# The same instructions of a routed-attention and SoLU kernel in another written-out order on every engine

## The chip, the cores and the metric

The kernel runs on one core of a Trainium2 chip. Its engines are TensorE (PE in the profile; its weight loads are shown apart as PEld), VectorE (DVE), ScalarE (ACT), GpSimd (POOL) and SyncE (SP), which here only issues transfers. The metric is the time of one execution on the device, in microseconds (us); smaller is better.

## What is computed

Attention in which a query sees only the keys of its own cluster, over 4 batches, 8 heads, 768 positions and head width 64, and behind it a feed-forward layer with a softmax gate on 3072 tokens (512 wide, 1024 inside):

```python
def _attn_ref(q, k, v, centroids):
    q_n, k_n, c_n = ...            # each row divided by its norm
    q_assign = np.argmax(np.einsum('bhsd,hcd->bhsc', q_n, c_n), axis=-1)   # 16 clusters
    k_assign = np.argmax(np.einsum('bhsd,hcd->bhsc', k_n, c_n), axis=-1)
    mask = q_assign[:, :, :, None] == k_assign[:, :, None, :]
    scores = np.where(mask, np.matmul(q, k.transpose(0, 1, 3, 2)) / np.sqrt(D), -1e9)
    attn = softmax(scores)
    return np.matmul(attn, v)

def _moe_ref(x, w_in, w_out, g_ln):
    h = x @ w_in
    solu = h * softmax(h)
    ln = (solu - mean(solu)) / np.sqrt(var(solu) + 1e-06) * g_ln
    return ln @ w_out
```

Inputs and output are float32; the large products run in bf16.

## The kernel before

The work is cut into named tasks, each of one engine. A task is added with what it needs and a function that issues its instructions. The engine's order is not found by a scheduler at build time: it is written out by hand as a text, `Weave.ORDER`, one per engine, in which a word such as `ld4` means the next four tasks of the kind `ld` on that engine, taken in the order in which they were added. Within a kind the order is fixed by that; the text sets only how the kinds are interleaved. `Weave.run` places the tasks so and issues them; every engine then works its own list strictly in order, and semaphores make it wait where an input isn't ready.

The kinds that matter below, with the lines of their instructions:

- On SP: `ld` loads of q and k (lines 381 and 406; from batch 1 on, four strips of 96 KB make one operand of a head pair), `lv` loads v of a head pair (line 536, 384 KB into tile `vf`), `lo` and `li` the weights (574, 558), `tx` transposes the attention output x of one or two row tiles into `xT` (704), `tu` transposes the gated activation u of a row tile into `uT` (760), `ou` stores a row tile of the output (827), `pl` places cluster rows (519).
- On PE: `wm` and `fl` are idle matmuls on a zeroed tile that nobody reads (844); `tp` turns the first batch's q and k (393); `cl` compares with the centroids (457 and 452); `S` is one bank of scores (615); `V` multiplies the exponentials with v (644); `h` and `y` are the two products of the feed-forward layer (736 and 800), each in four parts; `ptx` and `ptu` transpose by PE at the end (714, 724).
- On ACT: `E` is the exponential of one score bank (625), `ex` that of the feed-forward layer (748), `sc` scales the output (815 or 817), `xa` copies turned q and k out of PSUM (400).
- On DVE: `tb mx oh ot` find the cluster of each row (466, 479, 491, 501), `xt` turns q and k of later batches (414), `N` normalises attention output (669), `hm u bn ag` are the maximum, the gate and the variance of the feed-forward layer (742, 755, 766, 770).
- On POOL: `ca` and `cv` cast operands (440, 442, 541), `pl` and `bl` place and blank cluster rows, `at` and `al` make the scale of a row tile (776, 782, 785).

There are 24 row tiles of 128 tokens. Tile f goes through `h` (PE), `hm` (DVE), `ex` (ACT), `u` (DVE), `tu` (SP), `y` (PE), `sc` and `ou`. Scores run in a ring of three PSUM banks and their exponentials in a ring of nine tiles, `vf` has three buffers and `raw` (q and k as loaded) eight. Attention of later batches and the feed-forward layer of earlier ones are interleaved on all engines from about 40 us on.

Of the kernel before, what the change touches and what calls it, by code (L numbers as in the profile page):

```python
# [22 lines left out]
class Weave:  # L23
# [3 lines left out]

    ORDER = {}
    ORDER["SP"] = """
        ld4 si ld4 lg lv ld2 lv ld3 lo ld lv ld2 lv ld2 lo2 ld3 lo ld4 li ld li3 tx ld lv  # L30
        ld3 lv tx ld3 tu ld8 tu tx ld5 lv tu ld3 ou ld3 tu ou ld2 lv ld10 tu ld6 ou tx lv
        ld2 tu ld ou ld2 tx ld tu ld2 lv ld2 tx ld tu ou2 ld lv ld8 tu2 ld ou ld7 pl ou ld
        lv2 ld3 tu lv tx ou tu lv pl ld4 ou2 tx lv tu tx ou tu pl2 tu2 tx tu tx ou2 tx ou tu
        tx2 ou tu2 ou2 tu2 ou6
    """
    ORDER["POOL"] = """
        po zo ca3 z ca pl ca bl pl2 ca bl ca pl sg cv z ca3 cv ca pl cv pl2 ca2 pl gs pl2 cv
        ca z ca z2 cv ca2 pl3 ca2 pl cv pl3 ca bl ca wi4 cv at ca2 pl2 cv ca pl ca pl cv al
        at2 ca cv bl ca al ca pl al pl bl pl cv at pl ca4 at ca2 al ca pl2 bl pl2 cv2 ca3 al
        at pl2 bl pl2 ca pl al ca3 at cv at pl ca pl2 ca2 pl al cv2 bl cv2 pl2 ca pl al pl  # L40
        at al at pl2 ca3 at al bl cv pl2 bl cv2 ca3 pl5 al cv3 at al ca2 cv ca cv ca2 at ca2
        pl ca al pl2 at2 pl3 at ca cv al at2 al2 at2 al at al3 at al2 at2 al2
    """
    ORDER["PE"] = """
        fl wm fl tp2 cp fl2 cl tp fl tp fl4 cl S3 tp2 S cq tp S tp S tp S2 tp S tp S2 cl S2
        tp S V S V S V S gt V S V2 S cl S3 V3 S tp S tp S tp S2 tp V S V2 S2 cl S4 V S V3 S3
        V S V S V S V S cl S3 V3 S2 V S su S4 V2 S V S V su S4 V2 S V S V me S4 V2 ptx V2 S4
        cl S2 V2 S h S V S V S h3 S2 V2 S V S2 V h2 V S V S V S h S V S h S3 V S h S V3 h S
        V2 S h S h S2 y S y2 S y S V S V S V cl h S V S h S2 V2 S h2 S3 y4 V2 h V S V S h S
        V h V S h2 S y3 S2 y V3 h S3 cl V2 S V S y S2 y2 S3 V3 S y S2 V3 S2 cl S V S2 V2 S h  # L50
        S2 V2 S V S h S2 V2 cl V2 S3 y2 S V S2 V y S2 y V2 S3 h2 S V h S h S2 V h S V S V y2
        S h V y2 S2 V S h3 S cl V S2 V2 S h V cl S3 h2 V y V S3 y2 V S h V3 S y S h S2 h2 S3
        V2 y h S V S2 y V3 y S3 h3 y S3 V3 S h S V S V cl S V S h S cl V2 S3 y V2 S y S2 y
        V2 S3 h y V S3 V h V2 S3 cl S2 V2 S y3 S2 y S V3 S V S y S2 V S V3 S2 y2 S3 y V2 S2
        h V2 S3 h3 S V S2 V y S V h2 V2 S y S2 y V y S h2 S3 cl h V S2 V3 S h V2 S3 h2 S y
        S2 V h S2 V y2 V4 S3 y h S2 h V h V S V S y2 S3 V3 h2 S2 h2 S2 y2 S V S h2 S V3 S2 h
        S h S2 V S y V2 S V y2 S2 h2 S2 h2 V2 S2 V2 y S2 h V2 h V S2 h S V h S3 V2 h y S V
        y3 V h3 S2 y3 S2 y h2 V2 h y h y3 h V h V y4 h ptx h y4 h2 y3 h2 y ptu2 y6 ptu y ptu
        y5
    """  # L60
# [1240 lines left out]
```

## Time and profile before

| | |
|---|---|
| time, median of 3 runs | 222.88 us (222.58 to 223.67) |
| span of the profiled execution, first to last instruction | 221.0 us |
| what lies around the span, by the median | 1.9 us |
| PE busy | 213.4 us (97%) |
| DVE, ACT, POOL busy | 197.3, 191.0, 130.1 us (89%, 86%, 59%) |
| moved by DMA | 38.67 MB, mean 175 GB/s |

The listing gives the three times without saying which execution was profiled, so the span is set beside the median. A row of the profile names the line, the engine, the operation and out<-in by the program's tiles; times are from the span's start. SPq is SP's queue of issues: a row's length there is how long SP was held by the issue, not how long the transfer took.

### The profile page before, as it was taken

The page shows a single profiled execution, that of the slowest core. Times are in us where ns is not written, and L with a number is a line of the kernel's source. Part 1 is how long each engine was busy: PE and PEld are TensorE (multiplying, and loading weights), DVE is VectorE, ACT ScalarE, POOL GpSimd, SP SyncE. Part 2 cuts the span into 40 slices and gives each one's busy share as a digit, 9 for nine tenths or more (in the row PEclk, how much of TensorE's full clock was granted, in tenths as well). Part 3 has the DMA queues.
Part 4 walks back from the last instruction along what each step waited for, and adds up shares of the span by engine and source line. Part 5 has one row for each costly group of instructions (what it writes and reads, how often), then busy time and mean ns, then how long its engine had stood idle before and what let it go on. Part 6 is the DMA issues. An engine that isn't in the chain of part 4 may idle for free.

```text
span 221.0 us, 6580 instructions
## 1 busy us (share of the span) xinstructions
PE 213.4 (97%) x2392; PEld 148.3 (67%) x2424; DVE 197.3 (89%) x356; ACT 191.0 (86%) x372; POOL 130.1 (59%) x251
## 2 busy tenths in 40 slices
PE   7999999999999999999999999999999999999993
PEld 4667766767766687775677776777677677755452
DVE  3899998999999999998998989887999889888982
ACT  2799999989988999998899899999899998983363
POOL 3699989933845999637667634953895403022331
PEclk9999999999999999999999999999999999999999
DMA  6999988979999979999999896599930434396723
GB/s 147 346 279 236 281 197 223 274 159 164 176 175 209 192 157 141 204 215 176 202 221 162 189 177 169 123 210 208 237 59 19 89 63 130 90 134 169 176 78 142
DMA packets 125167, 38.67 MB, mean 175 GB/s; under 512 B 114504, under 2 KB 120656, under 8 KB 125136
## 3 DMA queue, kind: packets, MB, share of 16 engines
q1 hardware_dynamic: 123392, 37.73, 82.5%
q10 hardware_dynamic: 1744, 0.52, 1.0%
q8 instruction: 19, 0.31, 0.6%
q14 instruction: 12, 0.10, 0.1%
HBM read 23.11 MB, written 6.29 MB: 133 GB/s over the span
## 4 chain that ended last, share of the span: by engine, by line
PE 88%; DMA 3%; ACT 2%; DVE 2%; issue 2%; POOL 0%; ACTq 0%; DVEq 0%
PE sps L615 27%; PE yps L800 17%; PE hreg L736 16%; PE ops L644 15%; PE csc L457 4%; DMA uT<-u 3%; PE hreg L393 2%; ACT e L625 2%; PE idle_p L844 1%; PE hreg L615 1%; PE csc L452 1%; PE hreg L583 1%; PE hreg L800 1%; DVE u L755 1%; PE hreg L593 0%
## 5 line engine op out<-in xcount | busy, mean ns | idle before, releaser
L625 ACT ACTIVATE e<-sps 128x512 bf16<-128x512 f32 (+1 forms) x278 | 144.4, 609 | 9.6 <-PE sps L615 8.4
L615 PE MATMUL sps<-qk 80*128 80x256 bf16 (+5 forms) x616 | 92.4, 264 | 0.6 <-DVE qk L523 0.3
L615 PEld LDWEIGHTS <-qk 80*128 80x128 bf16 (+1 forms) x636 | 60.3, 121 | 25.7 <-issue 8.0
L644 PEld LDWEIGHTS <-e 128*128 128x128 bf16 x1134 | 50.0, 97 | 12.0 <-issue 1.9
L644 PE MATMUL ops<-v,e 128*128 128x65 bf16 x1134 | 55.0, 193 | 0.1
L736 PE MATMUL hreg<-w_in_sb,xT 128*128 128x512 bf16 x172 | 48.9, 379 | 1.2 <-issue 0.2
L800 PE MATMUL yps<-w_out_c,uT 128*128 128x512 bf16 x172 | 46.5, 379 | 0.9 <-DMA uT<-u 0.4
L523 POOL COPY qk<-oht 32x384 f32<-32x384 f32 (+1 forms) x48 | 24.0, 500 | 16.2 <-DVE oht L501 14.1
L755 DVE TENSOR_TENSOR u<-e_sb,hreg 128x1024 bf16<-128x1024 bf16 (+1 forms) x25 | 29.2, 1170 | 4.4 <-ACT e_sb L748 4.2
L748 ACT ACTIVATE e_sb<-hreg,nmax 128x1024 bf16<-128x1024 f32 x24 | 27.0, 1124 | 5.8 <-DVE nmax L742 5.7
L742 DVE TENSOR_REDUCE nmax<-hreg 128x1 f32<-128x1024 f32 x24 | 29.1, 1211 | 3.0 <-PE hreg L736 2.8
L766 DVE BATCH_NORM_STATS2 bs<-u 128x6 f32<-128x512 bf16 x48 | 31.5, 678 | 0.1
L800 PEld LDWEIGHTS <-uT 128*128 128x128 bf16 x200 | 18.3, 97 | 12.2 <-DMA uT<-u 0.5
L440 POOL CAST qk<-xt 64x768 bf16<-64x768 f32 (+1 forms) x30 | 24.4, 814 | 3.2 <-DVE xt L400 1.7
L442 POOL TENSOR_SCALAR qk<-xt 64x768 bf16<-64x768 f32 (+1 forms) x31 | 25.1, 809 | 2.0
L782 POOL TENSOR_SCALAR esq<-es,mv 128x1 f32<-128x1 f32 x24 | 8.7, 362 | 29.3 <-DVE mv L770 21.3
L736 PEld LDWEIGHTS <-xT 128*128 128x128 bf16 x192 | 16.7, 97 | 10.3 <-issue 1.3
L414 DVE STREAM_TRANSPOSE xt<-raw 128x768 f32<-128x768 f32 x24 | 22.6, 952 | 0.0
L669 DVE TENSOR_TENSOR x<-ops,den 128x256 bf16<-128x256 f32 (+1 forms) x39 | 18.9, 486 | 1.3
L776 POOL TENSOR_SCALAR es<-esum 128x1 f32<-128x1 f32 x24 | 5.3, 222 | 25.1 <-ACT e_sb L748 24.7
L541 POOL CAST v<-vf 128x384 bf16<-128x384 f32 x27 | 13.9, 528 | 5.6 <-DMA vf<-in_v_dram 4.9
L785 POOL TENSOR_TENSOR alpha<-esq,halves 128x1 f32<-128x1 f32 x24 | 13.7, 570 | 2.0
(86 smaller groups left out, 186.2 us busy)
## 6 DMA issues: line engine op xcount, KB each, us to landing
vf<-in_v_dram SPq DMA_DIRECT2D x16, 384.0 KB, 5.2
out_dram<-y SPq DMA_DIRECT2D x23, 256.0 KB, 2.6
raw<-in_q_dram SPq DMA_DIRECT2D x50, 96.0 KB, 3.5
raw<-in_k_dram SPq DMA_DIRECT2D x50, 96.0 KB, 3.5
w_g<-in_moe_w_out_dram SPq DMA_DIRECT2D x4, 512.0 KB, 6.5
w_st<-in_moe_w_in_dram SPq DMA_DIRECT2D x4, 512.0 KB, 5.8
raw<-in_q_dram SPq DMA_DIRECT2D x3, 384.0 KB, 6.1
raw<-in_k_dram SPq DMA_DIRECT2D x3, 384.0 KB, 6.6
```

The lines of the kernel that those rows point to most:

```text
L440: VEC[e].tensor_copy(dst, src)
L442: VEC[e].tensor_scalar(dst, src, scalar1=inv_C, scalar2=1.0, op0=Alu.mult, op1=Alu.mult)
L523: ins = VEC[e].tensor_copy(dst.bitcast(F32), src.bitcast(F32).unsqueeze(1) .to_broadcast([NB, 2, n // 2]))
L615: ins = nc.tensor.matmul(sps_[n, k][:, c0:c0 + w], side(b, h // 2, 1, h % 2, keys)[r], side(b, h // 2, 0, h % 2, slice(s0 * P, s0 * P + w) ...
L625: ins = nc.scalar.activation(es[n, k][:, :w], sps_[n, k][:, :w], Act.Exp, scale=exp_scale, bias=-exp_scale)
L644: nc.tensor.matmul(opss[g][:, s, :VW], es[n, k][:, c0:c0 + P], v1[slot(b, h // 2)][:, h % 2, kt, :VW], start=(kt == 0), stop=(kt == n_t - 1))
L736: uses(nc.tensor.matmul(hreg[:, at(f, f2)[1], :], xTs[f][:, dc, :], w_in_sb[:, dc, f2 * FF2:(f2 + 1) * FF2], start=(dc == 0), stop=(dc == ...
L742: uses(nc.vector.tensor_reduce(ff[f, "nmax"][:], pair_of(f), axis=AXY, op=Alu.max, negate=True), *both(f))
L748: uses(nc.scalar.activation(ff[f, "e"][:], pair_of(f), Act.Exp, bias=ff[f, "nmax"][:], accum_out=ff[f, "esum"][:]), *both(f))
L755: uses(nc.vector.tensor_tensor(ff[f, "u"][:, at_], ff[f, "e"][:, at_], pair_of(f)[:, at_], op=Alu.mult), *banks)
L766: nc.vector.bn_stats(ff[f, "bs"][:, f2, :], ff[f, "u"][:, f2, :])
L800: ins = nc.tensor.matmul(dst, ff[f, "uT"][:, at(f, f2)[0] * (n_fc // 2) + c, :], w_out_c[:, fc, cols], start=(fc == chunks[0]), stop=(fc = ...
```

## The change

Only the five texts of `ORDER` differ. The tasks, their functions, their needs, their engines, the tiles and the number of buffers are the same, so every engine has exactly the same instructions, in another order. The kinds' words stand for the same tasks in both, since within a kind on an engine the sequence is unchanged. Two lines of the diff, the start of SP's and of PE's text:

```diff
     ORDER["SP"] = """
-        ld4 si ld4 lg lv ld2 lv ld3 lo ld lv ld2 lv ld2 lo2 ld3 lo ld4 li ld li3 tx ld lv
...
+        ld4 si ld3 lv ld lg ld lv ld9 lv ld lo2 ld lv ld2 lo2 ld4 li4 ld tx ld3 lv ld2 tx lv
...
     ORDER["PE"] = """
-        fl wm fl tp2 cp fl2 cl tp fl tp fl4 cl S3 tp2 S cq tp S tp S tp S2 tp S tp S2 cl S2
...
+        fl8 wm tp2 cp tp cl tp cl fl S2 tp2 cq S3 tp2 S tp S2 tp S cl S2 tp S V gt S tp S2 V
```

**SP, around the transpositions of u of tiles 3 to 5.** The rows are SP's transfers in their order; `raw` is a strip of q or k, `vf` a load of v, `uT` and `xT` the transpositions, `out_dram` a store. Before, the piece begins with the load of v of pair 3 of batch 1 and the `uT` is that of tile 4, the `xT` that of tiles 6 and 7, and the last `uT` that of tile 5:

```order
L536 DMA vf<-in_v_dram 128x2x384
L406 DMA raw<-in_k_dram 32x24x32 x4
L406 DMA raw<-in_q_dram 32x24x32 x4
L406 DMA raw<-in_k_dram 32x24x32 x2
L760 DMA_TRANSPOSE uT<-u 128x8x128
L406 DMA raw<-in_k_dram 32x24x32 x2
L406 DMA raw<-in_q_dram 32x24x32 x4
L827 DMA out_dram<-y 128x512
L704 DMA_TRANSPOSE xT<-x 128x8x128
L536 DMA vf<-in_v_dram 128x2x384
L406 DMA raw<-in_k_dram 32x24x32 x2
L760 DMA_TRANSPOSE uT<-u 128x8x128
```

Now, from the load of the same v on; the first `uT` is that of tile 3, the second that of tile 4, and the `xT` of tiles 6 and 7 follows four strips behind the last row, the `uT` of tile 5 three strips behind that:

```order
L536 DMA vf<-in_v_dram 128x2x384 x2
L406 DMA raw<-in_q_dram 32x24x32
L827 DMA out_dram<-y 128x512
L406 DMA raw<-in_k_dram 32x24x32
L760 DMA_TRANSPOSE uT<-u 128x8x128
L406 DMA raw<-in_k_dram 32x24x32 x3
L406 DMA raw<-in_q_dram 32x24x32 x4
L536 DMA vf<-in_v_dram 128x2x384
L406 DMA raw<-in_k_dram 32x24x32 x3
L827 DMA out_dram<-y 128x512
L760 DMA_TRANSPOSE uT<-u 128x8x128
L536 DMA vf<-in_v_dram 128x2x384
```

Three loads of v (pairs 0, 1 and 2 of batch 2) have moved ahead of the transposition of x for tiles 6 and 7, and one strip of q has moved behind it. Two loads of v have moved ahead of the transposition of u of tile 5, and none behind.

**PE, at the start.** The idle matmuls write `idle_p`; `hreg<-ident_f,raw` turns q and k, `csc` compares with the centroids, `sps` is the first bank of scores. Before, from the last 512-wide idle matmul on:

```order
L844 MATMUL idle_p<-w_out_c 128x512
L844 LDWEIGHTS w_out_c
L844 MATMUL idle_p<-w_out_c 128x256
L393 MATMUL hreg<-ident_f,raw 128x128 x6
L890 MATMUL cps<-ident_f,w_in_sb 128x128
L844 LDWEIGHTS w_out_c
L844 MATMUL idle_p<-w_out_c 128x256
L844 LDWEIGHTS w_out_c
L844 MATMUL idle_p<-w_out_c 128x256
L457 MATMUL csc<-xt,c_bd 32x192 x4
L393 MATMUL hreg<-ident_f,raw 128x128 x3
```

Now, from the same matmul on:

```order
L844 MATMUL idle_p<-w_out_c 128x512
L393 MATMUL hreg<-ident_f,raw 128x128 x6
L890 MATMUL cps<-ident_f,w_in_sb 128x128
L393 MATMUL hreg<-ident_f,raw 128x128 x3
L457 MATMUL csc<-xt,c_bd 32x192 x4
L393 MATMUL hreg<-ident_f,raw 128x128 x3
L457 MATMUL csc<-xt,c_bd 32x192 x4
L844 LDWEIGHTS w_out_c
L844 MATMUL idle_p<-w_out_c 128x256
L615 LDWEIGHTS qk_99
L615 MATMUL sps<-qk_99 128x384
```

Eight of the nine 256-wide idle matmuls now stand at the head, ahead of the six 512-wide ones (before it was one ahead and one behind), and the first comparison with the centroids stands behind nine turns instead of six.

More of the change, by code (lines that the diff above doesn't have):

```diff
@@ L35 @@
+        ld2 tu ld8 tx tu ld3 lv ld3 tu ld ou ld4 lv2 ld ou ld tu ld7 lv ld3 ou tu lv ld4 tx
+        ld3 tu ld3 tx ou ld4 tu ld2 tx lv ld2 tu ld6 ou ld3 lv ou tu ld5 ou ld lv tu ld3 pl
+        tu ld ou lv ld ou tx lv tx ld ou tu ld pl ld pl ou tu tx tu2 pl ou tu ou tx tu tx ou
+        tx ou tx tu2 tx ou2 tu ou tu2 ou6
     """
     ORDER["POOL"] = """
-        po zo ca3 z ca pl ca bl pl2 ca bl ca pl sg cv z ca3 cv ca pl cv pl2 ca2 pl gs pl2 cv
-        ca z ca z2 cv ca2 pl3 ca2 pl cv pl3 ca bl ca wi4 cv at ca2 pl2 cv ca pl ca pl cv al
@@ L39 @@
[L39 to L42, printed above, removed]
+        po ca3 pl zo bl ca2 pl sg pl2 bl ca2 z ca cv2 ca2 cv ca pl2 ca pl ca gs ca2 pl ca
+        pl2 ca2 z ca pl cv pl2 z cv2 ca wi pl z pl wi pl wi2 pl2 cv ca bl pl ca pl ca at2 cv
@@ L43 @@
+        ca pl al ca cv ca al bl z ca cv ca2 cv pl at pl al pl bl at pl ca4 cv pl2 al at pl
+        cv2 pl bl ca al cv pl2 cv pl2 at al ca cv ca2 bl ca2 at ca pl2 ca pl2 ca bl ca al at
+        pl2 al ca cv2 pl3 at pl cv ca at cv ca pl bl ca cv at pl2 ca al ca pl cv2 ca pl al
+        ca bl pl3 ca al at ca2 at ca al cv ca pl ca cv pl al at pl ca pl2 ca cv ca pl at ca
+        al at2 al3 at3 al at al at al3 at al at al
     """
     ORDER["PE"] = """
-        fl wm fl tp2 cp fl2 cl tp fl tp fl4 cl S3 tp2 S cq tp S tp S tp S2 tp S tp S2 cl S2
@@ L46 @@
[L46 to L57, printed above, removed]
@@ new lines @@
+        S2 h S h S2 V2 h S3 V2 h S V2 y h S2 y2 S2 y S V4 S cl S V2 S2 h S h S2 cl V4 S3 y2
+        S2 y S y S2 V4 S3 h2 S h2 S3 V h y S V3 h S y S2 y h S y S h S V cl S2 h V5 cl S2 h
+        S h2 S3 h V3 y S2 h y S V3 y S2 y S h S2 V3 S2 h S y S2 V3 y2 S y S V2 h S3 V cl S2
+        V3 h S2 h S h S h S2 V2 S V2 cl S2 V S V y S y S2 V2 y S3 V h y S3 V3 h S2 h S cl S3
+        V y4 S3 V3 y2 S2 V2 S V2 S2 y S y S V4 S2 h2 S3 h2 S2 h S h S2 V6 S y2 S2 y S h S y
+        S V h S2 V cl S3 h2 y S V4 y S2 h2 S3 V3 y S y S V3 h2 S3 h2 S2 h S y S V4 y h S3 V2
@@ L71 @@
-        ag2 bn tx hm bn sc u bn ag hm bn tu ag u2 bn2 ag sc
+        cn xa cb ca tb mx oh ot pl2 tb mx oh ot cf xa3 cv xa2 tb xa mx oh gk ot ca N tb xa
+        mx pl xa oh ot xa N xt2 tb cv mx N tb pl oh ca ot N mx N oh pl N ot sk xt2 N ce2 tx
+        ce2 N ce2 N ce tb ce mx hm N oh u ot bn2 N hm xt2 u bn N ag hm bn sc xt u ag tb N xt
+        mx oh bn2 ot hm ag N xt cv u sc bn2 xt N tb mx xt oh hm ot N ag u bn sc bn xt2 N tb
+        hm tb cv N mx oh mx ag u ot oh bn N bn ag hm ot xt u xt N xt bn hm tb bn ag u mx tb
@@ L72 @@
+        N hm oh xt bn mx u N ot bn sc xt hm ag oh N u xt ot bl bn xt tb N mx bn oh hm bn ot
+        tb ag mx N u bn xt bn xt ag bn sc oh N tb hm ag sc N ot u mx N bn oh xt bn N ag ot
+        ca hm sc u N bn xt hm bn tb bl mx u N bl bn hm oh bn ag u ag ot N hm cv bl bn u bn2
+        hm N u ag N sc hm bn N bn u bn2 ag hm N ag u bn2 hm N bn ag u ag N hm bn2 u bn2 hm
+        sc u N bn ag tx ag hm bn sc u bn ag hm tu bn ag u2 bn2 ag sc
     """
     ORDER["ACT"] = """
-        wa xa3 pl ca E2 xa E8 pl E6 xa E11 xa E49 ex E10 ex E6 ca E4 ex E8 ex E3 sc E5 ca E2
@@ L75 @@
-        ex E25 ex E9 sc E6 ex E5 sc E2 ex E9 ex E8 ex E9 sc E6 ex E18 ex E21 ex E5 sc E3 ex
-        E9 ex E7 sc E2 ex E7 ex E8 ex E7 ex E6 sc E ex E2 sc E3 ex E2 sc ex sc ex sc ex tu
-        sc tu2 sc2 oz
+        wa xa3 ca pl E2 xa E5 pl E8 xa E12 xa E47 ca E3 ex E11 ex E8 ex E11 sc E3 ex E6 ca
+        E9 ex E13 ex E8 sc E6 ex E5 sc E2 ex E9 ex E12 ex E3 sc E12 ex E18 ex E18 ex E7 sc
+        E3 ex E9 ex E2 sc E5 ex E7 ex E8 ex E8 ex E2 sc E4 ex E3 sc E2 ex sc E3 ex sc ex sc
+        ex sc tu3 sc2 oz
```

22 lines of the change are left out of this document (7 added, 15 removed).

## The prediction

> **What bounds the kernel now.** I read the page's busy times and its chain of work first, then the chain piece by piece, then the stages, then SP's own queue.
>
> The page's span, its busy line, and the shares of the chain that ended last:
>
> ```profile
> span 221.0 us, 6580 instructions
> PE 213.4 (97%) x2392; PEld 148.3 (67%) x2424; DVE 197.3 (89%) x356; ACT 191.0 (86%) x372; POOL 130.1 (59%) x251
> PE 88%; DMA 3%; ACT 2%; DVE 2%; issue 2%; POOL 0%; ACTq 0%; DVEq 0%
> ```
>
> PE holds 88% of the chain, so no order can beat PE's own work by much. How much that is comes from pieces of the chain in which PE runs without a gap (start us, length us, what, number of matmuls):
>
> ```profile
> 58.54 0.86 PE yps L800 x4
> 61.30 0.78 PE csc L457 x8
> 65.59 0.66 PE sps L615 x6
> 165.36 0.73 PE ops L644 x24
> ```
>
> A matmul of the feed-forward products takes 0.215 us, one of the scores 0.11, one with v 0.030, a comparison of eight 0.78. Over the order that makes 192 x 0.215 = 41 for `h`, 41 for `y`, 636 score matmuls (36 banks of the last batch are cut in four, at half the length each) 62, 1152 x 0.030 = 35 for `V`, 17 comparisons 13, and some 14 for the turns, the weight sums and the idle matmuls: 206 us. The span is 15 us longer. About 3.3 of the 15 are the first matmuls at half pace, 2 more are waits before the first score, and 4 lie behind the last matmul, so waits inside the body can't be much over 5 us. That is the most that a new order can win; what it can lose has no such limit.
>
> The second resource is the transfer queue. Three stages (us, length, busy of each engine with its count, granted clock, DMA share, GB/s):
>
> ```profile
> 60.00:80.00 20.00, 19.68 (x217) 13.56 (x220) 19.29 (x34) 18.02 (x34) 13.28 (x26) 1.00 1.04 194
> 80.00:100.00 20.00, 19.43 (x253) 14.82 (x255) 19.32 (x37) 19.32 (x39) 13.41 (x25) 1.00 0.99 172
> 160.00:180.00 20.00, 19.74 (x246) 14.79 (x249) 17.53 (x30) 19.38 (x38) 11.24 (x22) 1.00 0.24 47
> ```
>
> Between 60 and 100 us the 16 DMA engines are full (1.04 and 0.99), at 160 they are not (0.24). And SP, which issues nearly all transfers, never rests there (start us, length us; `raw` is a strip of q or k, `vf` a load of v):
>
> ```profile
> 75.31 0.47 SPq L536 DMA_DIRECT2D vf<-in_v_dram  x1
> 75.83 4.92 SPq L406 DMA_DIRECT2D raw<-in_k_dram  x4
> 80.79 2.23 SPq L406 DMA_DIRECT2D raw<-in_q_dram  x4
> 83.07 1.42 SPq L406 DMA_DIRECT2D raw<-in_k_dram  x2
> 84.59 1.37 SPq L760 DMA_TRANSPOSE uT<-u  x1
> 86.01 1.20 SPq L406 DMA_DIRECT2D raw<-in_k_dram  x2
> 87.25 2.84 SPq L406 DMA_DIRECT2D raw<-in_q_dram  x4
> 90.13 0.60 SPq L827 DMA_DIRECT2D out_dram<-y  x1
> 90.83 1.28 SPq L704 DMA_TRANSPOSE xT<-x  x1
> 92.21 0.53 SPq L536 DMA_DIRECT2D vf<-in_v_dram  x1
> 92.79 1.03 SPq L406 DMA_DIRECT2D raw<-in_k_dram  x2
> 93.92 2.14 SPq L760 DMA_TRANSPOSE uT<-u  x1
> ```
>
> Each row begins within 0.15 us of the end of the one before. No transfer waits for its data: it waits for its turn on SP. So a transposition is issued when SP comes to it, and whatever is put ahead of it delays it. How close its readers stand (the issue to the landing of that `xT`, then the first matmul that reads it, then the `uT` of tile 5 and its reader, from the chain):
>
> ```profile
> L704 SPq DMA_TRANSPOSE xT<-x x1: 1281/1281/1281, 90.8 to 90.8; - x1
> DMA to landing us min/median/max: 3.5/3.5/3.5
> 94.73 0.81 PE L736 MATMUL hreg<-w_in_sb,xT 128*128 128x512 bf16 x3
> 93.92 5.55 DMA uT<-u
> 99.52 1.04 PE yps L800 x4
> L800 PE MATMUL yps<-w_out_c,uT 128*128 128x512 bf16 x172 | 46.5, 379 | 0.9 <-DMA uT<-u 0.4
> ```
>
> The `xT` issued at 90.83 lands at 94.3 and is read at 94.73: 0.4 us to spare. The `uT` of tile 5 is the only transfer of the body in the chain: it lands at 99.5, and PE waited for it about 0.5 us (the group of line 800 has 0.9 of idle time in all, 0.4 of it for `uT`).
>
> **The change, part by part.** All work is the same; only waits can differ. One execution was profiled, with a span of 221.0; the median of the runs is 222.88, so I add 1.9 to a span.
>
> *Loads of v moved ahead of transpositions (SP).* The `xT` of tiles 6 and 7 gets three `vf` ahead of it and loses one strip; the `uT` of tile 5 gets two `vf`. The price of a `vf`: at the 194 GB/s of the stage, 384 KB take 2.0 us, a strip of 96 KB 0.5. SP's rows give the bounds. At 75.31 the issue itself takes 0.47, which is all it costs if the queue has room; but the four strips behind it take 4.92 where the next four take 2.23, so it costs up to 0.47 + 2.69 = 3.2. The one at 92.21 holds the `uT` behind it for 2.14 where another takes 1.37. I take 2.0, between the ends and set by the stage's rate, since the queue was full in both rows. One stretch was not full:
>
> ```profile
> 80.00:82.00 2.00, 2.00 (x32) 1.75 (x31) 1.97 (x5) 1.85 (x4) 1.81 (x4) 1.00 0.36 58
> ```
>
> Here 2 x (1 - 0.36) = 1.3 us of transfer time went unused, and work moved ahead can fill it. So the `xT` lands at 94.3 + 3 x 2.0 - 0.5 - 1.3 = 98.5. Its reader stands 0.2 us earlier in PE's work (counted over the order with the four prices above), and 0.6 later for the start below: 95.1. PE waits 3.4 and is then 4.0 late. The `uT` of tile 5 lands at 99.5 + 2 x 2.0 - 1.3 = 102.2; its reader would come, without the old wait, at 99.0, stands 1.2 earlier in PE's work, and is 4.0 late: 101.8. PE waits another 0.4. Against before, where 0.5 was waited here, PE is 3.9 us late behind this place.
>
> The Trainium skill bears on this in two ways. "DMA: Bandwidth & Descriptors", section "Queues, rings and completion order", says that SP owns one ring on each of the DMA engines and that descriptors are taken in ring order; by that a `vf` ahead delays the transposition in full, as the rows behind 75.31 say. The same page's "Specifications" give about 358 GB/s as a core's share of the memory; by that figure a `vf` costs 1.1 us, an estimate, and the same sum would end at 224.3 instead of 226.1. The stage's 194 GB/s decides for me.
>
> Similar moves stand at the `uT` of tiles 3 and 4 (2 to 2.5 `vf`, stores and strips ahead), 6, 7 and 8. They are not further terms: a late PE gives the queue time, so only the largest lateness counts, and it stands at the places above.
>
> *Idle matmuls moved to the head (PE).* What stands there now (start us, length us):
>
> ```profile
> 1.17 3.17 PE L844 MATMUL idle_p<-w_out_c 128*128 128x256 bf16 x8 [1.17 <-DVE halves L848]
> 4.13 1.46 PE L393 MATMUL hreg<-ident_f,raw 128*128 128x128 f32 x6
> 7.11 0.49 PE L393 MATMUL hreg<-ident_f,raw 128*128 128x128 f32 x3
> 5.63 0.48 ACT L400 COPY xt<-hreg 128x384 f32<-128x384 f32 x1 [1.29 <-PE hreg L393]
> 6.09 0.60 PE L457 MATMUL csc<-xt,c_bd 128*32 128x192 f32 x8 [0.16 <-DVE c_bd L901]
> 8.95 0.65 PE L615 MATMUL sps<-qk 80*128 80x384 bf16 x3 [0.26 <-DVE qk L523]
> ```
>
> Eight matmuls with 3584 columns take 3.17, 0.88 us for 1000, twice the 0.42 of line 800: PE starts at half pace. Seven more of 256 columns add up to 7 x 0.23 = 1.6 us ahead of the turns. But six turns take 1.46 here and three take 0.49 at full pace, so six that start later take about 1.0 and win 0.45; the last idle matmuls come into the full pace too, which wins about 0.2 more; the two turns' copies on ACT and DVE then set the comparison, which had 0.35 us from the end of the turns. It comes 0.4 (if half of the idle matmuls run at full pace) to 1.6 us late; I take 0.6. From the comparison to the first score at 8.95 stands a chain of DVE steps that is the same in both. This 0.6 is not added to the 3.9: it is inside it, since it only moves the reader.
>
> The skill's "TensorE: Matmul & The Clock Gate", section "What's actually happening", has the clock open after some 3.4 us of activity, whatever the matmuls are. By that the opening comes at the same instant in both orders, which is the 0.6 and not the 1.6.
>
> *Scores, exponentials and the ring (PE and ACT).* ACT is 86% busy and its part of the chain is line 625:
>
> ```profile
> L625 ACT ACTIVATE e<-sps 128x512 bf16<-128x512 f32 (+1 forms) x278 | 144.4, 609 | 9.6 <-PE sps L615 8.4
> ```
>
> A bank of scores must be read within the time that PE needs for the next two; with 0.61 for the exponential and the hops some 1.1 us of PE work are wanted between a bank and the third behind it. Counted over the orders, 35 places have less before and 18 now, while 10 products with v stand within 1.2 us of their last bank now and none before. What is won has no row of its own: at most the 2% of ACT in the chain, 4.4 us, halved: 2.2; at least nothing, as the new close places take it back. I take 0.7, nearer the lower end because PE is 97% busy as it is.
>
> *The rest.* The tail from the last products on (`y` of tiles 21 to 23, line 800 from 211 us) has the same order on PE, and costs nothing new. DVE's and POOL's tasks around `hm` and `u` move by one or two places, behind an `ex` that takes 1.1 us on ACT; where that cover is gone it is one more DVE task, 0.5 to 0.9 us, and the reader of `u` stands 8 us away.
>
> **Sum.** Span 221.0 + 3.9 - 0.7 = 224.2; with 1.9 around it 226.1 us. That is 1.4% over 222.88. About 0.5%, 1.1 us, is what a measurement of this kernel can tell from no change.
>
> **The rivals.**
>
> *The loads of v are free, and the order is simply better (faster).* If a `vf` costs only its issue, 0.5 us, the `xT` lands at 94.3 + 1.5 - 0.5 - 1.3 = 94.0 and nobody waits; taking `vf` out from right before the `uT` of tile 5 then removes that wait, 0.5. With 0.6 lost at the start and 1.7 won at the scores: 221.0 + 0.6 - 0.5 - 1.7 = 219.4, or 221.3 us. For it speaks that DMA idled at 80 to 82 and that 18 close places are fewer than 35; against it the 4.92 behind the `vf` at 75.31. It decides from a price below 0.9 us on, where the `xT` no longer comes late. Chance 0.23.
>
> *Losses and gains cancel (no change).* At about 1.0 us for a `vf` PE is late by 1.1 to 1.5, the scores give it back: 222.9. The price would have to lie in a narrow band, so 0.17, most of it for errors on other terms.
>
> *PE's clock falls back.* Of the idle matmuls only one now stands between the second comparison and the first score, four before. If PE rests long enough there to fall to half pace, the first 3 us of scores take 1.5 more: 227.6 with the forecast. The chain leaves PE no more than about 1.5 us of rest there, so 0.03 of the chance of slower.
>
> **How the numbers follow.** Forecast, with the clock rival: 0.60, slower by over 0.5%. Faster 0.23, same 0.17. The forecast's own range: with a `vf` at 1.1 the sum is 224.3; with 2.4 and nothing filled at 80 to 82 it is 229. Below it the range must take in most of the faster rival, down to 221.0, since 0.40 lies below 224; above 229 I leave out less than 0.1.
>
> **What would show it.** Right: in the profile after, a `uT<-u` or `xT<-x` between 75 and 105 us with several us in the chain; PE idle before line 736 or 800 there with a DMA named; SP's rows still without gaps to 100 us; the first score at about 9.5. Wrong: the span at 221 or less with no DMA in the chain, the strips behind the paired `vf` taking 0.55 each.

## The result, and the profile after

| | before | after |
|---|---|---|
| time, median | 222.86 us (222.58 to 223.67, 5 runs) | 229.10 us (228.36 to 229.93, 5 runs) |
| span of the profiled execution | 221.0 us | 227.8 us |

The ratio is 1.0281, 95% interval 1.0255 to 1.0307: 6.3 us slower. The direction was forecast; the size was not: 226.1 was said, with 229.0 as the upper end. The profiled execution of after is the longest of its five (229.93), so its rows add up to 6.8 us and not to 6.3.

The page of the kernel after, its span, busy times and the engines' shares of the chain that ended last:

```profile
span 227.8 us, 6617 instructions
PE 217.1 (95%) x2424; PEld 148.9 (65%) x2424; DVE 198.8 (87%) x356; ACT 192.3 (84%) x372; POOL 129.2 (57%) x251
PE 63%; DVE 20%; DMA 7%; POOL 4%; ACT 3%; issue 2%; SPq 0%; ACTq 0%; DVEq 0%; POOLq 0%
```

PE fell from 88% of the chain to 63%, DVE came up from 2% to 20%, DMA from 3% to 7%. So no one resource took over: the chain, which follows PE back while PE works and leaves it where PE rests, changes engines more often. PE's rows in the timeline of after with over 0.3 us of rest behind 30 us (start us, length us; the rest and what ended it in brackets):

```profile
34.21 1.19 PE L644 MATMUL ops<-v,e 128*128 128x65 bf16 x24 [0.92 <-DVE x L669]
73.57 1.04 PE L800 MATMUL yps<-w_out_c,uT 128*128 128x512 bf16 x4 [0.46 <-DMA uT<-u]
84.43 0.61 PE L800 MATMUL yps<-w_out_c,uT 128*128 128x512 bf16 x2 [0.34 <-DVE nmax L742]
99.42 1.04 PE L736 MATMUL hreg<-w_in_sb,xT 128*128 128x512 bf16 x4 [0.58 <-DMA xT<-x]
123.10 0.59 PE L800 MATMUL yps<-w_out_c,uT 128*128 128x512 bf16 x2 [0.94 <-DVE y L817]
136.95 0.59 PE L800 MATMUL yps<-w_out_c,uT 128*128 128x512 bf16 x2 [0.63 <-DVE cst L466]
```

Before had one such row (0.40, at 99.5). These six add up to 3.9 us, each under 1 us and hardly two of one kind. The third is really a transposition: PE's weight load there waited 0.46 us for `uT` of tile 3.

To see where time goes between such rows, take PE's order from its weight loads (all 2424 are in the trace), add up the prediction's prices over it, with 0.11 us for a turn of q or k, and ask at equal work done how much later PE is than before. The table has that in us, as the mean over 2 us around each time and good to about 0.2; the last line is read from the rows of the tail below. The other columns are kernels of the experiments:

| time in before | after | head48 | early_ou45 | head48_ou | dve_fix |
|---|---|---|---|---|---|
| 24 | 2.1 | 0.2 | 1.7 | 0.4 | 1.5 |
| 43 | 3.6 | 0.2 | 3.3 | 0.4 | 2.3 |
| 69 | 3.4 | 0.8 | 3.0 | 1.1 | 2.0 |
| 104 | 4.6 | 3.0 | 4.0 | 2.5 | 3.3 |
| 116 | 4.7 | 3.0 | 4.1 | 2.6 | 3.3 |
| 134 | 6.7 | 5.0 | 4.4 | 2.9 | 5.4 |
| 192 | 6.3 | 4.5 | 3.9 | 2.4 | 4.9 |
| 208.84 | 6.1 | 4.4 | 3.8 | 2.2 | 4.7 |

So after loses 3.6 us ahead of 43 us, 1.2 more from 69 to 104, 2.0 between 116 and 134, and wins 0.6 back from there to the tail. Of the 3.6, 2.1 stand at 24 us already; some 0.5 of those belong to this one execution, whose first score came late (see the last section). At the end the identical piece of the tail (six matmuls of line 800) stands at 208.84 in before and 214.95 in after, 6.1 later:

```profile
214.95 1.46 PE L800 MATMUL yps<-w_out_c,uT 128*128 128x512 bf16 x6
221.17 0.60 PE L800 MATMUL yps<-w_out_c,uT 128*128 128x512 bf16 x2 [0.22 <-ACT uT L732]
```

Another 0.4 is lost at the second row: on ACT the scaling of tile 21 now stands ahead of the copy of the turned `u` of tile 22. The last 0.3 is lost behind the last matmul; its cause stays open.

### The profile page after: what moved, and what is told of

It is laid out like the page before. It is cut to its first block, busy times and chain, and to the rows that moved or that the text cites. A ratio compares the mean times of both kernels' runs of the same rounds, so it can differ in the third digit from the quotient of the medians.

```text
span 227.8 us, 6617 instructions
## 1 busy us (share of the span) xinstructions
PE 217.1 (95%) x2424; PEld 148.9 (65%) x2424; DVE 198.8 (87%) x356; ACT 192.3 (84%) x372; POOL 129.2 (57%) x251
## 4 chain that ended last, share of the span: by engine, by line
PE 63%; DVE 20%; DMA 7%; POOL 4%; ACT 3%; issue 2%; SPq 0%; ACTq 0%; DVEq 0%; POOLq 0%
PE sps L615 17%; PE yps L800 14%; PE hreg L736 13%; PE ops L644 9%; PE csc L457 3%; DVE w_out_c L596 2%; DMA raw<-in_q_dram 2%; DMA w_g<-in_moe_w_out_dram 2%; DVE xt L414 2%; DVE nmax L742 2%; PE idle_p L844 2%; DVE cst L466 2%; PE hreg L393 2%; DVE oh L491 2%; DMA xT<-x 1%
## 5 line engine op out<-in xcount | busy, mean ns | idle before, releaser
L615 PE MATMUL sps<-qk 80*128 80x256 bf16 (+5 forms) x616 | 91.0, 263 | 1.1 <-DVE qk L523 0.5
L615 PEld LDWEIGHTS <-qk 80*128 80x128 bf16 (+1 forms) x636 | 63.4, 120 | 36.8 <-issue 6.9
L736 PE MATMUL hreg<-w_in_sb,xT 128*128 128x512 bf16 x192 | 53.6, 379 | 0.7 <-DMA xT<-x 0.6
L800 PE MATMUL yps<-w_out_c,uT 128*128 128x512 bf16 x184 | 50.4, 379 | 2.6 <-DVE y L817 0.9
L644 PE MATMUL ops<-v,e 128*128 128x65 bf16 x1134 | 50.0, 193 | 1.1 <-DVE x L669 0.9
L644 PEld LDWEIGHTS <-e 128*128 128x128 bf16 x1134 | 45.6, 97 | 6.2 <-DVE x L669 2.1
L800 PEld LDWEIGHTS <-uT 128*128 128x128 bf16 x200 | 17.4, 97 | 13.3 <-issue 2.2
```

The costliest lines, as they stand in the source:

```text
L615: ins = nc.tensor.matmul(sps_[n, k][:, c0:c0 + w], side(b, h // 2, 1, h % 2, keys)[r], side(b, h // 2, 0, h % 2, slice(s0 * P, s0 * P + w) ...
L644: nc.tensor.matmul(opss[g][:, s, :VW], es[n, k][:, c0:c0 + P], v1[slot(b, h // 2)][:, h % 2, kt, :VW], start=(kt == 0), stop=(kt == n_t - 1))
L736: uses(nc.tensor.matmul(hreg[:, at(f, f2)[1], :], xTs[f][:, dc, :], w_in_sb[:, dc, f2 * FF2:(f2 + 1) * FF2], start=(dc == 0), stop=(dc == ...
L800: ins = nc.tensor.matmul(dst, ff[f, "uT"][:, at(f, f2)[0] * (n_fc // 2) + c, :], w_out_c[:, fc, cols], start=(fc == chunks[0]), stop=(fc = ...
```

## The experiments

Four theories are set against each other. Q is the forecast's: the transpositions behind loads of v set PE's lateness, whatever was lost ahead of them. W is its wider form: SP's queue decides from 66 us on. By E the orders of the other engines lose the time, and the losses add. S puts the loss behind 116 us on the stores of y.

Times are medians; the ratio is to the runs of before on the same chip, with its 95% interval. A difference of two ratios, in us below, is good to about 0.7 to 1.1 us.

| kernel | us | ratio |
|---|---|---|
| sp_only | 243.29 | 1.0881 (1.0800 to 1.0962) |
| head_before | 230.46 | 1.0349 (1.0290 to 1.0408) |
| head_after | 226.12 | 1.0136 (1.0074 to 1.0199) |
| small_v | 228.36 | 1.0235 (1.0218 to 1.0252) |
| early_ou4 | 231.28 | 1.0342 (1.0307 to 1.0377) |
| sp_fix | 234.55 | 1.0502 (1.0474 to 1.0529) |
| dve_fix | 228.21 | 1.0222 (1.0192 to 1.0252) |
| both_fix | 234.56 | 1.0528 (1.0500 to 1.0556) |
| early_ou45 | 227.18 | 1.0185 (1.0145 to 1.0225) |
| head48 | 227.72 | 1.0198 (1.0165 to 1.0231) |
| tail_after | 226.94 | 1.0161 (1.0130 to 1.0192) |
| before_tu5 | 222.91 | 0.9980 (0.9960 to 1.0000) |
| head48_ou | 225.61 | 1.0110 (1.0072 to 1.0148) |
| head48_ou_lv | 225.13 | 1.0095 (1.0059 to 1.0132) |
| best | 223.98 | 1.0044 (1.0021 to 1.0066) |

Most of these times lie outside or between the ranges that had been expected. Inside one are small_v (theory E), head48_ou (the parts add) and before_tu5 (no change); head_after missed theory E by 0.1. So most of what follows rests on rows of the profiles and on differences between kernels.

**SP's order alone (sp_only).** The kernel before with SP's text of the change, first line:

```diff
-        ld4 si ld4 lg lv ld2 lv ld3 lo ld lv ld2 lv ld2 lo2 ld3 lo ld4 li ld li3 tx ld lv
+        ld4 si ld3 lv ld lg ld lv ld9 lv ld lo2 ld lv ld2 lo2 ld4 li4 ld tx ld3 lv ld2 tx lv
```

> The order of before on PE, DVE, ACT and POOL, and SP's order of the change. Theory Q (the forecast's: the three loads of v ahead of the x of tiles 6 and 7 make PE wait there): that x lands near 98 to 99, its reader stands at 94.7, PE waits 3.5 to 4.5 us in front of line 736, the time is 226 to 227.5 us. Theory E (the engines' orders, not SP's, lose the time: DVE's order up to 36 us and the scalings behind POOL's placements later): SP's order loses under 1 us, the time is 222.5 to 224.

20 us slower, and not for the forecast's place: no row of line 736 has a rest over 0.24 us. SP's rows at 161 us and PE's at 81, 163 and 180, in the timeline of this run:

```profile
81.26 1.03 PE L800 MATMUL yps<-w_out_c,uT 128*128 128x512 bf16 x2 [2.31 <-DMA uT<-u]
...
161.61 0.58 SPq L406 DMA_DIRECT2D raw<-in_k_dram  x1
163.00 1.03 PE L800 MATMUL yps<-w_out_c,uT 128*128 128x512 bf16 x2 [6.05 <-DMA uT<-u]
175.33 0.59 SPq L519 DMA_DIRECT2D qk<-oht  x1
...
180.06 1.04 PE L800 MATMUL yps<-w_out_c,uT 128*128 128x512 bf16 x2 [3.93 <-DMA uT<-u]
```

The longest rest, 6.05 us, waits for a `uT` that SP issued at 158.87: ahead of it SP had stood 4.9 and 5.1 us at two loads of v (issued at 145.57 and 155.71), whose buffers POOL's casts freed late. Then SP stood from 162.2 to 175.3 us at a placement of cluster rows whose data the other engines made late, and the next `uT` had to wait behind it: 3.93 us. An order of SP is only as good as its match with the orders that make its data; taken alone it can't be priced. The rest at 81 us is the forecast's mechanism, though: the `uT` of tile 3 behind two loads of v.

**The change behind before's head (head_before, head48), and the reverse (head_after).** Every engine runs one order up to a point of the program and from there the other's tasks that are not done, in the other's order. SP's first lines in head48, against those of the change:

```diff
-        ld4 si ld3 lv ld lg ld lv ld9 lv ld lo2 ld lv ld2 lo2 ld4 li4 ld tx ld3 lv ld2 tx lv
-        ld2 tu ld8 tx tu ld3 lv ld3 tu ld ou ld4 lv2 ld ou ld tu ld7 lv ld3 ou tu lv ld4 tx
+        ld4 si ld4 lg lv ld2 lv ld3 lo ld lv ld2 lv ld2 lo2 ld3 lo ld4 li ld li3 tx ld lv
+        ld5 tx lv ld2 tu ld8 tx tu ld3 lv ld3 tu ld ou ld4 lv2 ld ou ld tu ld7 lv ld3 ou tu
...
```

> Every engine runs the order of before up to the first sum of weights on PE (some 31 us), and from there the order of the change. Theory Q: the delay is set by the transfers at 95 us, what was lost ahead of them is covered: 228 to 229.5. Theory E, losses add up: the 2.5 us that PE had lost by 36 us are won back in full: 226 to 227.

> The reverse: the order of the change up to the first sum of weights (some 35 us), the order of before from there. Theory E: the 2.5 us lost up to there stay: 225 to 226. Theory Q: they stay as well unless some wait behind absorbs them; 0.5 of them is taken from the wait for the u of tile 5 (landing later than PE by less): 224.5 to 225.5. Against before it prices the head alone.

> Every engine runs the order of before up to the first product of the feed-forward layer (46 to 48 us), the order of the change from there. At that point PE is on time in before and 2.9 us late in the change. Theory W (from 66 us on the transfers decide when PE goes on): PE waits again for u of tile 2 at about 73 us and for later ones, and what was won is gone: 228 to 229.3. Theory E, losses add: 226 to 226.8.

head_before put its seam where the stall at 34 us is, and lost 2.0 us at the seam itself (scores waiting for POOL's placements), so it decides little: it still waits 1.5 us for `uT` of tile 2 and 2.1 for tile 7's bank. head_after keeps 1.4%, 3.0 us (1.7 to 4.4): the head is a cost of its own. But its profiled execution is 4.4 us late and lost 2.8 of them between 24 and 36 us, around its seam, with a lower clock (below), so it does not price the change's head. head48 has a later seam, where PE is 0.2 late instead of 3.6, and ends 1.9 us under after by the ratios: nearly half of the 3.4 is gone again. About 1 us of that is a rest at the seam itself (0.96 at 45.81, for DVE's normalisation). PE's rows of head48 show the rest of it, at the very places of the forecast:

```profile
96.67 1.04 PE L736 MATMUL hreg<-w_in_sb,xT 128*128 128x512 bf16 x4 [0.82 <-DMA xT<-x]
101.28 0.60 PE L800 MATMUL yps<-w_out_c,uT 128*128 128x512 bf16 x2 [1.22 <-DMA uT<-u]
```

**Three loads of v made small (small_v).** In the change:

```diff
-        nc.sync.dma_start(out=vf[:].rearrange("p h t d -> p h (t d)"), ...)
+        n = 16 if b == 2 and p < 3 else P        # in cast_v too
+        nc.sync.dma_start(out=vf[:n].rearrange("p h t d -> p h (t d)"), ...[:n])
```

> The change with the loads and casts of v for pairs 0 to 2 of batch 2 cut to 16 of 128 partitions (48 KB in place of 384; the rest of v is not loaded for these, all else is the same). Theory Q: the x of tiles 6 and 7 lands by 3 x 1.5 to 2.0 us earlier, at 93 to 95, PE's delay goes by what sits there: 225.5 to 226.5. Theory E: PE is late by 3 us before it gets there, so only its wait of 0.7 goes: 228 to 229.

1.0 us under after by the ratios; a part of that may be PE's start, below. The load's price comes out of SP's rows, first of after, then of small_v, where the two rows of `vf` begin the stretch and the `xT` ends it:

```profile
75.64 0.98 SPq L536 DMA_DIRECT2D vf<-in_v_dram  x2
78.28 3.65 SPq L760 DMA_TRANSPOSE uT<-u  x1
96.17 1.23 SPq L704 DMA_TRANSPOSE xT<-x  x1
```

```profile
75.05 0.98 SPq L537 DMA_DIRECT2D vf<-in_v_dram  x2
91.13 1.65 SPq L406 DMA_DIRECT2D raw<-in_q_dram  x3
93.76 1.23 SPq L706 DMA_TRANSPOSE xT<-x  x1
```

20.53 us in after, 18.71 in small_v, of which SP stood idle 0.98 ahead of the `xT` (its data came last, not its turn). The difference of 20.53 and 17.73 is 2.8 us for three loads with 7/8 of their bytes gone: 1.07 us for the bytes of a load of 384 KB. Six more profiles with the same order of SP here took 20.09 to 20.51 for the stretch, so the price is 0.9 to 1.07. It is that of the bytes: the small loads still hold SP for 0.49 each, so a whole load can cost up to 0.5 more. PE's rest in front of line 736 is gone.

**The stores of y (early_ou4, early_ou45).** What ended at 123 us: `y` of tile 6 is scaled on DVE into a buffer that still held the output of tile 4. From after, that store's time to landing in the view of its tile, and in the timeline SP's row of it and the scaling:

```profile
DMA to landing us min/median/max: 2.7/2.7/2.7
```

```profile
119.50 0.47 SPq L827 DMA_DIRECT2D out_dram<-y  x1
...
122.30 0.75 DVE L817 TENSOR_SCALAR y<-yps,alpha 128x512 f32<-128x512 f32 x1 [1.80 <-PE sps L615]
```

119.50 + 2.7 = 122.2. The bracket names a matmul that was long done; what DVE waited for was the store. PE's `y` of tile 7 needs the same single PSUM bank (`yps` and the comparisons `csc` share it), so PE waits behind DVE. The store's own data were ready at 99.0 (the scaling on ACT at 98.28 takes 0.69), but its turn on SP came 20.5 us later. Before, SP came to the same store at 109.99, and it landed 2.0 us ahead of the scaling of tile 6; SP's row, the time to landing and DVE's row of before:

```profile
109.99 1.43 SPq L827 DMA_DIRECT2D out_dram<-y  x1
DMA to landing us min/median/max: 3.5/3.5/3.5
115.47 0.74 DVE L817 TENSOR_SCALAR y<-yps,alpha 128x512 f32<-128x512 f32 x1
```

In SP's text of the change, and with both stores moved:

```diff
-        ld3 tu ld3 tx ou ld4 tu ld2 tx lv ld2 tu ld6 ou ld3 lv ou tu ld5 ou ld lv tu ld3 pl
+        ld3 tu ld3 tx ou ld4 tu ld2 tx ou2 lv ld2 tu ld9 lv tu ld5 ou ld lv tu ld3 pl tu ld
```

> The change with one store moved: the output of tile 4 goes ten transfers earlier in SP's order, to right ahead of the load of v of pair 3 of batch 2. In the trace of the change this store landed at 122.2 us, the scaling of tile 6 on DVE (which writes into its buffer) began at 122.3 and PE's first part of y of tile 7 at 123.1 after 0.94 us of rest. If the store is what PE waited for: that wait goes and 0.9 us with it, 228.2. If something else was late there (the scale on POOL, DVE itself): the wait stays, 229.1.

> The change with the stores of tiles 4 and 5 both moved ahead of the load of v of pair 3 of batch 2 (in the run with only the first moved, PE's rest of 0.94 us at 123 went, but the scaling of tile 7 waited for the store of tile 5, landed at 129.0, and PE then rested 2.9 us at a comparison that needs the same bank). Theory S (the stores of y are what was late between 119 and 130): both rests go, 227.5 to 228.3. If the queue's lateness only moves on to the next transposition (u of tile 7 or 8): 228.8 to 229.5.

With one store moved, the rest at 123 went and a longer one came, at a comparison that waits for the scaling of tile 7 and so for the store of tile 5 (issued at 123.47 right behind a load of v, 5.5 us to its landing). PE in early_ou4:

```profile
129.80 1.51 PE L457 MATMUL csc<-xt,c_bd 128*32 128x384 f32 x8 [2.94 <-ACT y L815]
```

With both moved, both rests are gone, and the only one left there is for the bank of tile 8 (134.59, 0.31). 2.1 us under after by the ratios, and the step of 2.0 between 116 and 134 us in the table shrinks to 0.3. With the head's 1.9 this is the largest cause that a run showed, and the one whose chain of waits is seen row by row.

**Transpositions ahead of the loads of v (sp_fix), DVE's order (dve_fix), both.** SP's first changed line, and DVE's two places:

```diff
-        ld2 tu ld8 tx tu ld3 lv ld3 tu ld ou ld4 lv2 ld ou ld tu ld7 lv ld3 ou tu lv ld4 tx
+        ld2 tu ld8 tx tu ld3 tu lv ld4 ou ld4 tu lv2 ld ou ld8 tu lv ld3 ou tx lv ld7 tu ld3
-        mx pl xa oh ot xa N xt2 tb cv mx N tb pl oh ca ot N mx N oh pl N ot sk xt2 N ce2 tx
+        mx pl xa oh ot xa N xt2 tb cv mx N tb pl N oh ot ca mx N oh pl N ot sk xt2 N ce2 tx
-        N hm oh xt bn mx u N ot bn sc xt hm ag oh N u xt ot bl bn xt tb N mx bn oh hm bn ot
-        tb ag mx N ...
+        N hm oh xt bn mx u N ot bn sc xt hm ag oh N u xt ot bl bn xt tb N mx bn oh hm tb bn
+        ot ag mx N ...
```

> The change with only SP's order mended at five places: the transpositions of u of tiles 2, 3 and 4 and of x of tiles 6 and 7 each go ahead of the load of v that stood before them, and the store of tile 4 as in the run above. Theory W (from 66 us on SP's queue decides when PE may go on): PE's rests at 73, 84, 99 and 123 us go (0.5, 0.5, 0.6, 0.9): 226.5 to 227.3. Theory E (the other engines' orders set the time): 228.3 to 229.2, only the store's share goes.

> The change with only DVE's order mended at two places: the normalisation that PE's products wait for at 34 us goes three tasks earlier, and the turn of the comparison of pair 1 of batch 3 goes ahead of two tasks, so that y of tile 8 finds its bank at 136 us. Theory E, losses add: 1.1 and 0.6 off, 227.2 to 227.6. Theory W: what is won at 34 us is waited for at SP's queue again, only 0.6 stays: 228.3 to 229.

> The change with both mends. Theory W: with the queue out of the way the loss at 34 us counts too, so the two together give more than the sum of each alone: 224.3 to 225.5. Theory E: the sum of the two runs above, 226.3 to 227.3.

sp_fix is 5 us slower than after, and no theory had that. Two of SP's rows, and two rests of PE:

```profile
87.37 0.86 PE L615 MATMUL sps<-qk 96*128 96x256 bf16 x3 [2.36 <-ACT e L625]
...
91.71 1.94 SPq L827 DMA_DIRECT2D out_dram<-y  x1
97.04 1.23 SPq L704 DMA_TRANSPOSE xT<-x  x1
...
107.99 1.03 PE L800 MATMUL yps<-w_out_c,uT 128*128 128x512 bf16 x2 [3.53 <-DMA uT<-u]
```

The `xT` was moved to where its data were not there yet: SP stood 3.4 us at it (93.65 to 97.04), and all that stood behind came later, the `uT` of tile 5 most of all. The rest at 87 us began in the same way: SP had stood 0.7 and 0.8 us at the `uT` of tiles 2 and 3, a strip of q behind them landed at 83.0 (in after at 81.7), and DVE, ACT and PE waited each for the one ahead. A part of the 5 us is a lower clock (below). So sp_fix doesn't test theory W, and both_fix with it doesn't either. dve_fix changes DVE's order alone (with the normalisation, a cast goes behind the `ot` next to it): 1.3 us under after by the ratios, with the stall at 34 us halved, between the ranges of both theories. The stall's making, DVE in after:

```profile
30.45 1.06 DVE L485 TENSOR_TENSOR w_out_c<-cst,mx 128x384 bf16<-128x384 f32 x1
31.55 1.07 DVE L442 TENSOR_SCALAR qk<-xt 64x768 bf16<-64x768 f32 x1
32.64 0.98 DVE L498 STREAM_TRANSPOSE w_out_c<-w_out_c 128x768 bf16<-128x768 bf16 x1
...
33.73 0.42 DVE L669 TENSOR_TENSOR x<-ops,den 128x256 bf16<-128x256 f32 x1
```

Three instructions of 1 us stand ahead of the normalisation that frees the bank of PE's next products with v. In dve_fix PE's rest there is 0.50 and now ends with POOL's cast of v.

**Both large parts taken away (head48_ou), and a load of v moved (head48_ou_lv).**

```diff
-        lv ld4 tx ld3 tu ld3 tx ou ld4 tu ld2 tx lv ld2 tu ld6 ou ld3 lv ou tu ...    (head48)
+        lv ld4 tx ld3 tu ld3 tx ou ld4 tu ld2 tx ou2 lv ld2 tu ld9 lv tu ...          (head48_ou)
+        ld4 tx ld3 tu lv ld3 tx ou ld4 tu ld2 tx ou2 lv ld2 tu ld9 lv tu ...          (head48_ou_lv)
```

> The order of before up to the first product of the feed-forward layer, the order of the change from there, and the stores of tiles 4 and 5 ahead of the load of v of pair 3 of batch 2. If the parts of the loss add: 227.7 less the 1.9 that the stores gave in the change, 225.5 to 226.2; what is left is the waits for x of tiles 6 and 7 (0.8) and u of tile 5 (1.2), u of tile 2 (0.4) and the bank of y of tile 8 (0.7). If the queue's lateness only moves on to another place: 226.8 to 227.7.

> The run above with one more move: the load of v of pair 2 of batch 2 goes behind the transposition of u of tile 5 (from ahead of the x of tiles 6 and 7). A load of v at 1.1 us: PE's two rests of 0.8 and 1.2 shrink by 1.1 in sum, 0.9 stay, the time is 1.1 under the run above. At the forecast's 2.0: both rests go, 2.0 under it. If something else holds these transpositions (their data, not the queue): no change.

These two parts add, within the intervals: 1.9 for the head and 2.1 for the stores make 4.0, and the two together give 3.8 by the ratios (1.0281 less 1.0110). The last move gives 0.3 to 0.5 us within wide intervals, and its profiled execution is the longest of its runs; it does not price the load. In head48_ou PE came to line 736 later than in head48 (0.75 and 0.46 us of rest at tiles 2 and 3), and no rest was left there to win. Up to 105 us head48 and head48_ou have the same order, so this difference, and the 3.0 against 2.5 at 104 us in the table, is one between two executions: half a us between two profiles shows no cause.

**The rest: tail_after, before_tu5, best.** tail_after has before's order up to `y` of tile 7 and the change's from there; before_tu5 moves one load; best joins before_tu5 with the change's order from tile 12 to 20.

```diff
-        ld3 lv tx ld3 tu ld8 tu tx ld5 lv tu ld3 ou ld3 tu ou ld2 lv ld10 tu ld6 ou tx lv
-        ld2 tu ld ou ld2 tx ...
+        ld3 lv tx ld3 tu ld8 tu tx ld5 lv tu ld3 ou ld3 tu ou ld2 lv ld10 tu ld6 ou tx ld2
+        tu lv ld ou ld2 tx ...
```

> Every engine runs the order of before up to the first part of y of tile 7 (116.6 us there), the order of the change from there. In the change PE lost 0.9 at y of tile 8 by DVE's order and won 0.6 back between 130 and 190, and lost 0.5 at the very end. If its order behind 117 us is no worse once the queue is not behind: 222.3 to 223.7. If that stretch costs by itself what it cost in the change (1.0 to 2.0): 224 to 225.

> The kernel before with one transfer moved: the load of v of pair 0 of batch 2 goes behind the transposition of u of tile 5 (three places later). In the trace of before PE rested 0.4 to 0.6 us for that transposition. If the load ahead of it delays it by about 1.1 us: PE's rest goes, 222.4 to 222.7. If the rest is set by DVE's u instead: no change.

> The kernel before with the load of v of pair 0 of batch 2 behind the transposition of u of tile 5 (which gave 0.5 us of rest), the order of the change on every engine from the first product of tile 12 (150 us) to that of tile 20 (195 us), where PE's lateness against before shrank from 5.8 to 5.4 us, and the order of before from there. If both gains are kept: 222.1 to 222.5. If the seams cost what they win: 222.6 to 223.5.

tail_after lost 3.5 us at its seam (125 us, scores waiting 1.98 for a placement on POOL, and a lower clock behind it), and has no verdict on the order behind it. before_tu5 took PE's rest of 0.4 away (no row of PE with over 0.25 us of rest behind 10 us is left) and is 0.2% faster, with the interval's end at no change. It is the fastest of all, inside what can be told from no change. best is 0.4% slower than before; its profiled run shows one rest of 0.29 us behind a seam and a span of 221.3, and why its other runs were longer stays open.

**A rest can cost more than itself.** In six kernels the clock that PE was granted (1.00 is full pace) fell around a rest. The stretches are 125 to 130 us of tail_after, 130 to 135 of early_ou4 and 30 to 40 of head_after (start and end, length, busy time of PE, PEld, DVE, ACT and POOL with its count, granted clock, DMA share, GB/s):

```profile
125.00:130.00 5.00, 4.71 (x36) 3.44 (x37) 2.76 (x7) 2.64 (x5) 4.51 (x11) 0.66 1.15 224
130.00:135.00 5.00, 5.00 (x42) 2.91 (x35) 2.28 (x5) 3.31 (x8) 3.92 (x8) 0.70 1.01 219
30.00:35.00 5.00, 4.18 (x46) 2.71 (x50) 4.55 (x9) 4.43 (x9) 3.89 (x10) 0.81 1.02 209
35.00:40.00 5.00, 5.00 (x54) 2.40 (x55) 2.31 (x6) 3.45 (x7) 4.58 (x8) 0.85 1.00 347
```

Counted as in the table, PE fell back by 3.5 us around the rest of 1.98 in tail_after, by 4.3 around that of 2.94 in early_ou4, and by 2.8 in head_after, whose rests there are 0.64 and 0.17. In sp_only the clock fell to 0.50 (160 to 165 us), and its rests of over 0.24 us add up to 14.2 of the 19.7 us by which PE is late at the tail; in sp_fix PE fell back by 8.7 from 80 to 104 us with rests of 5.9. both_fix has 0.50 from 105 to 110. It does not always happen: rests of 1.99 and 2.06 in head_before left the clock at 1.00, and how long a rest must be is not shown. In the profiles of before, after, head48, early_ou45, head48_ou, dve_fix and small_v it is 1.00 in every 5 us from 10 to 220 us, so the table is free of it.

## Why the prediction was wrong, point by point

**The loads of v ahead of `xT` and `uT`: right place, wrong price, and not where PE lost the time.** Forecast were landings at 98.5 and 102.2. From after's chain (start us, length us):

```profile
96.17 3.20 DMA xT<-x
99.42 1.04 PE hreg L736 x4
```

The `xT` landed at 99.4; the `uT` of tile 5 was issued at 99.31 and landed at 102.7. PE's lateness behind this place was 4.6, forecast 3.9. That these are near each other is luck, since two errors cancelled in the landings. The price of 2.0 us for a load was too high: its bytes measured 0.9 to 1.07. The Trainium skill's "DMA: Bandwidth & Descriptors", section "Specifications", has the figure of some 358 GB/s a core, which gives 1.1 us a load as an estimate. small_v comes near it; the prediction had set it aside for the stage's 194 GB/s. With 1.07 the `xT` would land at 94.3 + 3.2 - 0.5 - 1.3 = 95.7. The other 3.7 us are mostly SP's own lateness, which the sum took as that of before. SP had stood at the first `xT` until its data came, from after and then before (the idle time is the gap between rows):

```profile
36.60 0.65 SPq L406 DMA_DIRECT2D raw<-in_q_dram  x1
42.02 1.29 SPq L704 DMA_TRANSPOSE xT<-x  x1
```

```profile
35.31 1.48 SPq L558 DMA_DIRECT2D w_st<-in_moe_w_in_dram  x3
38.46 1.35 SPq L704 DMA_TRANSPOSE xT<-x  x1
```

4.8 us against 1.7. At the load of v of pair 3 of batch 1 SP is level again (75.64, in before 75.31), but with the `uT` of tile 3 and a store still to come, which before had behind it and which held SP for 3.65 and 0.48 us here. How much of the 1.3 us of unused queue time was filled is not shown. "No transfer waits for its data: it waits for its turn" held from 75 to 101 us, where the rows were read, and not ahead of it.

And PE did not lose 3.9 there: by the table's count it came 4.3 late and waited 0.58, where the forecast had it 0.6 late and waiting 3.4. Where it came earlier, 1.3 late (head48), it waited 0.82 and 1.22, 2.0 in sum: the size that the mechanism has with a load at 1.1 us, for which the prediction gave 224.3.

**"Only the largest lateness counts, and it stands at the places above": the step that failed.** A part of it held: of the 3.4 us that head48 saves ahead of 43 us, the waits at these places took some 1.0 back. But behind 104 us after lost 2.0 more. The stores of y had been seen moving ("stores and strips ahead") and not been followed to who waits for them: buffer of y, scaling, PSUM bank, PE. early_ou45 shows 2.1 us for it, and head48_ou that it adds to what was lost ahead.

**"The rest": costed at 0.5 to 0.9 a place and then at nothing.** DVE's order cost at 34 us and at 137 us; dve_fix gives 1.3 back. The products with v and the bank of `yps` had no cover, and were not looked at. This is the other half of the failed step: the forecast put PE 0.6 us late ahead of its place, and PE was 3.6 late at 43 us.

**The start: 0.6, right.** By the time from the span's start the first score begins at 8.8 to 9.6 us in the nine profiles that start with before's order, middle 9.2, and at 9.4 to 10.3 in the eight with the change's, middle 9.8. But it was counted as "inside the 3.9"; it is part of the 3.6 that the head costs in this execution; taking the head away in head48 gave 1.9 at the end.

**The scores: 0.7 won, not shown.** In the stretch without other losses lateness falls by 0.6 (from 134 us to the tail), about the size that was said. But best, which has the change's order from 150 to 195 us, won nothing by it, so that the 0.6 comes from the scores stays open.

**The tail: nothing said, 0.7 found** (0.4 at the copy on ACT, 0.3 behind the last matmul). PE's order there is the same, as was said; ACT's is not.

**The rivals.** That loads of v are free is refuted (0.9 to 1.07 each for the bytes alone). That losses and gains cancel is refuted. The clock did not fall back in after (1.00, above). What of the 6.3 us no run assigned: head48_ou still is 2.5 us over before; its rows show rests of 0.96 at the seam, 0.75 and 0.46 at tiles 2 and 3, 0.56 at a comparison (106.28), 0.29 at tile 8, and the tail's 0.7, but none of them was taken away alone.

## What to carry to other kernels

In an order written for engines that run strictly in sequence, follow each moved transfer to the last one who waits for it: a store frees a buffer, the buffer a bank, and the bank lets PE go on; here two stores in a late place cost 2.1 us, twice what taking the bytes of three loads of v away gave (1.0). A transfer's best place has two sides: later than its data are ready, since the queue stands still until they are (3.4 us in sp_fix), and ahead of large transfers that nobody needs yet. Where a change reorders everything, sum up the lateness of the critical engine from stage to stage. Ask at each stage whether its wait is for something that comes at a fixed time, which absorbs what was lost ahead (some 1.0 of 3.4 us in head48), or adds to it (the stores).

## What was not expected of the hardware

PE's full pace began at a different time from run to run with the same start. The first six turns in after and in small_v, which have the same order:

```profile
5.41 1.49 PE L393 MATMUL hreg<-ident_f,raw 128*128 128x128 f32 x6
```

```profile
5.31 0.82 PE L393 MATMUL hreg<-ident_f,raw 128*128 128x128 f32 x6
```

Both began to work at 1.17 us; one made the turns at half pace, 1.49, the other at full pace, 0.82, and the first score begins at 10.31 in after, at 9.48 in small_v, for no reason of the order. Over the eight profiles with this start, the first turn at full pace came 4.1 us (there the first turn of all) to 5.9 us after PE's first matmul. The Trainium skill's "TensorE: Matmul & The Clock Gate", section "What's actually happening", names some 3.4 us and says that the number of slow matmuls varies with the run. These eight profiles have it later, and with a spread of 1.8 us.
